# First q as fp32 by SyncE with a cast on chip, X of the last two batches turned by transposing DMAs, last stores on two queues, a new order

## The chip, the cores and the metric

The kernel runs on one core of a Trainium2 chip. The time is that of one execution on the device, in microseconds (us); lower is better. Of the kernel before there are three runs, and one profiled execution, from which the rows below are taken.

## The reference, cut to what matters

There are B = 4 batches of H = 8 heads, S = 768 tokens in 8 blocks of 96, and D = 64 columns a head. A matrix of 8x8 per head, normalised five times over rows and columns, mixes the blocks of k and v; each block of q then attends to one mixed block. The result x, with the heads side by side 512 wide, goes through a token mixer.

```python
for _ in range(5):                                  # sort_net, [B, H, 8, 8]
    P = exp(P - max(P, -1)); P = P / sum(P, -1); P = P / sum(P, -2)
k_sorted = einsum('bhij,bhjcd->bhicd', P, k_b)      # and v_sorted
attn = softmax(q_b @ k_sb^T / 8)                    # inside a block of 96
x = (attn @ v_sb), heads side by side               # [B, 768, 512]
wq, wk = x @ w_q, x @ w_k                           # 64 wide
mixed = (wq @ wk^T / 8) @ x
out = relu(mixed) @ w_out
```

## The kernel before, in words

The whole program is written out as units, and a string ORDER sets the order in which they are issued. A unit is a letter, a batch and a number: `P21:4` is unit P of batch 2, number 1, in PSUM bank 4. A capital letter is TensorE's work (PE in the rows); a small letter is the work that takes a bank away or stands between, with the engine behind the colon: A is ScalarE (ACT in the rows), D is VectorE (DVE), G is GpSimd (POOL), S is SyncE (SP). Each engine works its own units off in the order of the string, and stands still where the next one is not ready. The first lines of the string do the normalising (a, c, with B and n spreading the result to the mixing matrices M) and filling matmuls on zeros (Z). A batch then goes through these steps:

- lq, lk, lv load a whole batch of q, k or v: fp32 in memory, bf16 in the tiles Qn, Kn, Vn, the cast being done by the DMA. GpSimd issues them (L230). lp loads w_q and w_k (into a part of an output tile, until U and z have turned them), lo loads w_out.
- Q turns q of two heads, K mixes and turns k, V mixes v; q, k, v (small) copy the results to QT, KT and Vs. For batch 0 v goes through Y, y, F and f.
- R: six DMAs on SyncE's queue (L313) carry Vs to VT in another layout. All P units of the batch need all six.
- S and e are scores and exp, P the product with v, r and x the reciprocal (L375) and the division that writes X (L380). X has five parts, x0 to x4, of 14 (the last of 8) head-and-block units out of 64.
- T turns X of two heads with 8 matmuls against an identity, and t copies that to XT (the helper's L159 or L161): four units of each kind in a batch.
- J projects XT with w_q and w_k, j copies it to qkT, d copies half of its rows to qD (L407). W and w turn the part of w_k, G and g form w_k^T x, H and h the mixed rows with relu (L443 or L445), O is the product with w_out, o copies it to an output tile `ot`, and s stores it (L468, L471).

Four output tiles `ot` go round; two XT tiles and two X tiles alternate with the batches. SyncE's DMAs are issued one after the other in the order of the string, each when what it reads is there.

Of the kernel before, what the change touches and what calls it, by code (L numbers as in the profile page):

```python
# [17 lines left out]
ORDER = """
i02:D lq0 i00:G c00:D a01:A c01:D A00:0 a02:A:0 c02:D a03:A Z07:0 Q00:0 c03:D Q01:1 a04:A c04:D
q01:D:1 lk0 a05:A Q03:7 Q02:6 c05:D Z08:1 B00:1 n01:D:1 n00:D:1 Z04:2 K00:2 K01:4 q00:A:0 k00:A:2  # L20
n02:D:1 u00:D:1 i03:G n03:D:1 K03:0 K02:2 k01:A:4 k02:D:2 k03:A:0 S00:4 S02:0 e00:A:4 q02:D:6 lv0
e02:A:0 Y02:2 q03:D:7 Y01:4 lv1 Y00:6 y01:D:4 Y03:0 y02:A:2 S04:2 y00:A:6 n10:G n11:G y03:D:0 S03:4
F01:6 F00:7 e04:A:2 S01:0 F03:2 e03:A:4 e01:A:0 f01:D:6 f00:D:7 V11:3 V12:5 f03:D:2 F02:7 P00:0
v11:A:3 lk1 v12:D:5 S05:2 f02:A:7 e05:A:2 r00:D:0 V10:4 n21:G P01:6 K13:2 x00:D:0 r01:D:6 P02:0
x01:D:6 v10:A:4 r02:D:0 K10:4 K12:6 k13:A:2 P03:2 x02:D:0 lq1 r03:D:2 k10:A:4 K11:4 k12:D:6 T01:0
T00:1 lp Q11:6 k11:A:4 t00:A:1 S06:4 U00:7 R12:S Q12:1 R15:S e06:A:4 R11:S x03:D:2 P04:2 t01:D:0
Q13:0 Q10:4 q11:A:6 r04:D:2 z01:A:7 S12:5 q12:D:1 x04:D:2 q13:A:0 U01:7 q10:D:4 z02:D:7 T02:1 T03:0
e12:A:5 t02:D:1 t03:D:0 lq2 S11:2 S10:4 S13:6 Q22:1 Q21:0 e11:A:2 q21:D:0 Q23:2 e10:A:4 q22:D:1
J00:3 e13:A:6 R10:S R14:S n20:G R13:S S16:4 e16:A:4 S15:0 j00:D:3 P11:6 S14:3 J01:5 e15:A:0 q23:D:2
e14:A:3 P12:0 r11:D:6 lk2 K23:2 j01:A:5 x11:D:6 K21:6 r12:D:0 P13:4 k23:A:2 K20:2 x12:D:0 k21:A:6  # L30
r13:D:4 n30:G K22:0 Q20:6 x13:D:4 W00:7 k20:A:2 lv2 k22:A:0 P14:2 lq3 V20:4 V22:0 d00:S q20:D:6
r14:D:2 W01:7 x14:D:2 V21:2 T12:6 v22:D:0 t12:D:6 v20:A:4 P10:4 S25:0 v21:A:2 S26:2 T13:6 r10:D:4
w00:A:7 T11:7 x10:D:4 d01:S e26:A:2 S23:2 n31:G e25:A:0 Q30:4 G00:5 S21:0 t13:D:6 e23:A:2 t11:D:7
S24:6 lk3 e21:A:0 G01:5 Q31:3 lv3 e24:A:6 g00:D:5 Q33:2 q31:D:3 S22:0 T10:5 e22:A:0 S20:6 q33:D:2
t10:D:5 K32:2 R21:S K31:0 J11:5 k32:A:2 R20:S q30:D:4 R22:S H00:2 Q32:4 e20:A:6 k31:D:0 lo j11:D:5
h00:A:2 R23:S K30:0 R24:S H01:6 q32:D:4 K33:4 h01:A:6 R25:S k30:D:0 P21:2 J10:0 V31:6 k33:A:4 P23:4
j10:A:0 v31:A:6 r21:D:2 P22:0 d10:S x21:D:2 r23:D:4 V32:2 W10:6 v32:A:2 W11:6 O01:7 x23:D:4 w10:A:6
V30:4 r22:D:0 v30:A:4 x22:D:0 o01:D:7 O02:2 S34:0 o02:D:2 H02:6 e34:A:0 h02:D:6 S32:3 O03:5 e32:A:3
o03:A:5 P20:0 T21:7 P24:2 r20:D:0 T22:4 t21:A:7 G10:5 G11:5 x20:D:0 r24:D:2 d11:S g10:D:5 S36:6
R32:S t22:A:4 S30:0 e36:A:6 R35:S O00:4 x24:D:2 S31:5 e30:A:0 R30:S H11:2 H10:0 O05:7 o00:D:4 T20:4  # L40
h11:D:2 o05:D:7 e31:A:5 R34:S T23:5 h10:A:0 t20:A:4 t23:A:5 S35:2 e35:A:2 R31:S S33:0 H12:6 e33:A:0
s01:S O04:4 J20:5 O10:3 s00:S j20:A:5 R33:S P31:0 J21:5 o10:A:3 P32:2 h12:D:6 O15:6 r31:D:0 o04:D:4
j21:A:5 r32:D:2 o15:A:6 x31:D:0 P33:4 r33:D:4 O12:7 o12:A:7 P30:0 x33:D:4 s02:S O13:6 d20:S P34:4
W20:7 x32:D:2 W21:7 r34:D:4 d21:S o13:A:6 T31:2 w20:D:7 O14:3 t31:D:2 r30:D:0 O11:7 G20:2 x30:D:0
G21:2 o11:A:7 s10:S x34:D:4 T30:7 o14:A:3 g20:A:2 t30:A:7 T32:0 T33:1 t32:D:0 t33:D:1 H21:4 H20:2
H22:6 h20:D:2 s11:S J30:0 J31:1 h22:D:6 O20:2 j30:D:0 O21:3 h21:A:4 W30:0 O22:7 j31:A:1 d31:D
w30:A:0 W31:0 o22:D:7 w31:D:0 O24:1 o20:A:2 o21:A:3 o24:A:1 G30:7 G31:7 g30:D:7 O23:0 d30:D H30:4
h30:A:4 o23:D:0 H31:2 s12:S h31:D:2 O25:7 s20:S H32:0 s21:S O31:4 o25:A:7 h32:D:0 O30:7 o31:D:4
s22:S s31:S O314:0 O34:1 o314:A:0 s314:S o34:A:1 o30:D:7 O32:4 O35:0 o32:A:4 s30:S o35:A:0 s34:S
s32:S O315:7 o315:A:7 s315:S s35:S O33:4 o33:A:4 s33:S  # L50
"""


# [638 lines left out]
```

## Time and profile before

| what | us |
|---|---|
| median of three runs (lowest, highest) | 109.45 (108.54, 109.75) |
| span of the profiled execution, first to last instruction | 107.8 |
| PE busy | 89.2 |
| DVE busy | 72.2 |
| ACT busy | 68.6 |
| POOL busy | 25.6 |

The profile gives no other time for the profiled execution than its span. The median of the runs lies 1.65 us above that span, which stands for what lies around it. An engine's busy time counts its own instructions and not those that issue DMAs.

### The profile page before, as it was taken

Reading aid. Unit: us, or ns where it says so; the run is one execution under the profiler, and the core shown is the slowest. Engines: PE = TensorE matmul, PEld = TensorE weight load, DVE = VectorE, ACT = ScalarE, POOL = GpSimd, SP = SyncE. Lnnn points to the kernel's source line nnn. Section 1 sums busy time; section 2 is a strip of 40 time slices with the busy share of each in tenths; the row PEclk is TensorE's granted clock in tenths of the full one; section 3 lists DMA queues with packets and bytes.
Section 4 is the critical chain, followed back from the end, with each engine's and each line's share of the span. In section 5 each row is a group of like instructions: output and inputs, shape, how many; then the busy total and the mean of one; then the engine's idle time right before and its main releaser. Section 6 shows DMA issues by size and latency. Waiting matters only on the chain.

```text
span 107.8 us, 3532 instructions
## 1 busy us (share of the span) xinstructions
PE 89.2 (83%) x1495; PEld 63.0 (58%) x1503; DVE 72.2 (67%) x143; ACT 68.6 (64%) x99; POOL 25.6 (24%) x42
## 2 busy tenths in 40 slices
PE   0296997899989399989977799999999999999600
PEld 0126556798868377888845675856666755445300
DVE  2675655879987458979568499687299795587000
ACT  4223009999879848969959489999842664252600
POOL 5950009699089600000000000000000560000000
PEclk9999999999999999999999999999999999999995
DMA  0999999799999999999999933816060292447391
GB/s 3 106 197 205 203 203 205 81 191 205 209 236 247 223 199 204 209 209 205 236 253 223 179 78 102 270 70 222 6 231 0 78 406 109 198 179 270 121 376 39
DMA packets 18882, 19.37 MB, mean 180 GB/s; under 512 B 944, under 2 KB 17200, under 8 KB 18864
## 3 DMA queue, kind: packets, MB, share of 16 engines
q0 software_dynamic: 13296, 10.09, 61.7%
q1 hardware_dynamic: 5568, 9.03, 24.4%
q8 instruction: 12, 0.20, 0.7%
q14 instruction: 6, 0.05, 0.1%
HBM read 20.19 MB, written 6.29 MB: 246 GB/s over the span
## 4 chain that ended last, share of the span: by engine, by line
PE 50%; DMA 26%; ACT 7%; DVE 4%; POOL 4%; issue 3%; ACTq 0%; POOLq 0%; DVEq 0%
PE ps L155 50%; DMA Kn<-in_k_dram 19%; DMA Qn<-in_q_dram 7%; ACT E L351 3%; POOL M L251 2%; ACT KT L159 2%; DVE KT L161 2%; DVE M L251 1%; DVE QT L161 1%; POOL Vn L230 1%; POOL Qn L230 1%; ACT VT L159 1%; ACT ot L159 1%; DVE PTR L161 0%; ACTq L159 0%
## 5 line engine op out<-in xcount | busy, mean ns | idle before, releaser
L351 ACT ACTIVATE E<-ps 96x960 bf16<-96x960 f32 (+1 forms) x28 | 23.8, 909 | 3.1 <-PE ps L155 2.9
L155 PE MATMUL ps<-wo,mixT 128*128 128x512 bf16 (+1 forms) x97 | 22.8, 362 | 0.5 <-issue 0.2
L380 DVE TENSOR_TENSOR X<-ps,Rall 96x896 bf16<-96x896 f32 (+1 forms) x20 | 19.8, 1000 | 0.5
L159 ACT CAST KT<-ps 128x768 bf16<-128x768 f32 x14 | 10.7, 810 | 7.4 <-PE ps L155 7.3
L159 ACT COPY ot<-ps 128x512 f32<-128x512 f32 (+2 forms) x18 | 9.4, 541 | 8.4 <-PE ps L155 7.7
L155 PEld LDWEIGHTS <-mixT 128*128 128x128 bf16 x104 | 9.0, 98 | 8.3 <-issue 1.0
L155 PE MATMUL ps<-VT,E 96*128 96x65 bf16 x256 | 11.3, 193 | 1.4 <-ACT KT L159 1.3
L155 PEld LDWEIGHTS <-E 96*128 96x128 bf16 x256 | 9.9, 97 | 3.5 <-issue 1.6
L483 POOL CROSS_LANE_REDUCE s<-Rall 96x1 f32<-96x280 f32 x1 | 0.8, 757 | 46.8 <-DVE Rall L375 46.8
L155 PE MATMUL ps<-idb,Qn 128*64 128x128 bf16 x192 | 8.5, 244 | 3.1 <-DMA Qn<-in_q_dram 3.0
L251 POOL TENSOR_TENSOR M<-PTR,m_p 128x512 bf16<-128x512 bf16 x6 | 7.8, 1314 | 13.4 <-DVE PTR L161 9.5
L155 PEld LDWEIGHTS <-KT 64*128 64x128 bf16 (+1 forms) x288 | 8.4, 97 | 3.6 <-issue 2.2
L155 PEld LDWEIGHTS <-Qn 128*64 128x64 bf16 x192 | 7.2, 126 | 4.7 <-DMA Qn<-in_q_dram 4.2
L155 PE MATMUL ps<-QT,KT 64*128 64x96 bf16 x256 | 9.1, 204 | 0.7 <-ACT KT L159 0.7
L445 DVE TENSOR_SCALAR mixT<-ps 128x1024 bf16<-128x1024 f32 x7 | 8.5, 1221 | 1.2 <-PE ps L155 0.7
L161 DVE COPY QT<-ps 128x768 bf16<-128x768 bf16 x13 | 6.9, 547 | 3.3 <-PE ps L155 3.2
L375 DVE RECIPROCAL Rall<-ps 96x14 f32<-96x14 f32 (+1 forms) x20 | 4.6, 230 | 5.9 <-PE ps L155 4.7
L155 PE MATMUL ps<-M,Kn 128*64 128x128 bf16 x192 | 7.5, 221 | 1.1 <-DMA Kn<-in_k_dram 0.8
L159 ACT CAST Vs<-ps 128x1024 bf16<-128x1024 f32 x7 | 7.1, 1016 | 1.5 <-PE ps L155 1.5
L155 PE MATMUL ps<-fil 128*128 128x512 bf16 x18 | 6.5, 506 | 1.8 <-ACT m_p L173 1.6
L155 PEld LDWEIGHTS <-Kn 128*64 128x64 bf16 x192 | 6.1, 109 | 2.4 <-DMA Kn<-in_k_dram 0.9
L161 DVE COPY ot<-ps 128x512 f32<-128x512 f32 x9 | 6.0, 679 | 2.0 <-PE ps L155 2.0
(81 smaller groups left out, 132.7 us busy)
## 6 DMA issues: line engine op xcount, KB each, us to landing
out_dram<-ot SPq DMA_DIRECT2D x9, 512.0 KB, 3.1
Qn<-in_q_dram POOLq DMA_DIRECT2D x4, 768.0 KB, 11.4
Kn<-in_k_dram POOLq DMA_DIRECT2D x4, 768.0 KB, 12.7
Vn<-in_v_dram POOLq DMA_DIRECT2D x4, 768.0 KB, 15.1
VT<-Vs SPq DMA_DIRECT2D x18, 132.0 KB, 6.3
out_dram<-ot SPq DMA_DIRECT2D x4, 256.0 KB, 3.4
wo<-in_moe_w_out_dram POOLq DMA_DIRECT2D x1, 512.0 KB, 26.8
out_dram<-ot SPq DMA_DIRECT2D x4, 128.0 KB, 2.3
```

The lines of the kernel that those rows point to most:

```text
L155: nc.tensor.matmul(o, w, x, is_transpose=t, start=start, stop=stop, skip_group_check=True)
L159: nc.scalar.copy(o, i)
L161: nc.vector.tensor_copy(o, i)
L230: nc.gpsimd.dma_start(out=t[b % NIN][:, h0:h1].rearrange("p h r d -> p h (r d)"), in_=src[b, h0:h1].rearrange("h (p r) d -> p h (r d)", p=P))
L251: ENG[e].tensor_tensor(out=M[b % 2][:, h0:h0 + hn], in0=src.unsqueeze(2).to_broadcast([P, hn, SP, NB]), in1=m_p.unsqueeze(1).unsqueeze(3). ...
L351: nc.scalar.activation(E[b % 2][:, n, 0:2 * w * BLK].rearrange("p (t a c) -> p a t c", a=2, c=BLK), PS[0:BLK, bank:bank + 2, 0:w * BLK].re ...
L375: nc.vector.reciprocal(Rall[:, b, n, :, 0:w], avps(bank, w)[:, :, :, D])
L380: nc.vector.tensor_mul(xo.rearrange("p (a t d) -> p a t d", a=2, d=D), avps(bank, w)[:, :, :, 0:D], Rall[:, b, n, :, 0:w].unsqueeze(3).to_ ...
L445: nc.vector.tensor_relu(o, i)
L483: g.tensor_reduce(s1[:, 1:2], rv, axis=AX.XYZWC, op=ALU.max)
```

## The change

- Two DMAs on SyncE's queue bring q of batch 0 as fp32, four heads each, into the two XT tiles, which nothing else uses yet. Four units z1 cast two heads each into Qn: z10, z11 and z12 on GpSimd, z13 on ScalarE. The unit lq0 is gone.
- Batches 2 and 3 have no T and t units any more (eight of each). Units D20, D21, D30 and D31 are transposing DMAs on SyncE's queue instead: each turns half of X (four heads: 96 partitions x 16 pieces of 128 columns, bf16) into half of XT. D20 and D30 read parts x0 to x2, D21 and D31 read x2 to x4.
- Three of the last eight stores (s34, s35, s30) are issued by ScalarE.
- The order is new. Fewer Z matmuls stand in it: 9 and 6 where there were 7, 8 and 4. lp stands ahead of the first k.

```diff
-SPQ = False
+SPQ = 2
 ORDER = """
-i02:D lq0 i00:G c00:D a01:A c01:D A00:0 a02:A:0 c02:D a03:A Z07:0 Q00:0 c03:D Q01:1 a04:A c04:D
+i00:G A00:6 i02:D c00:D lp a01:A c01:D Z09:0 lk0 i03:G z10:G z11:G Q01:2 lv0 a02:A:6 c02:D Q00:3
...
-s32:S O315:7 o315:A:7 s315:S s35:S O33:4 o33:A:4 s33:S
+o314:D:6 s35:A o32:D:4 o31:A:7 o33:D:2 O30:6 s315:S s314:S s32:S o30:A:6 s33:S s31:S s30:A
 """
...
     if SPQ:
-
-        q32 = XT[0].rearrange("p t s -> p (t s)").bitcast(FP32).rearrange("p (h r d) -> p h r d", r=R6, d=D)
-        nc.sync.dma_start(out=q32.rearrange("p h r d -> p h (r d)"),
-                          in_=q[0, 0:H // 2].rearrange("h (p r) d -> p h (r d)", p=P))
+        q32 = [x.rearrange("p t s -> p (t s)").bitcast(FP32).rearrange("p (h r d) -> p h r d", r=R6, d=D) for x in XT]
+        for m in range(SPQ):
+            hs = slice(m * H // 2, (m + 1) * H // 2)
+            nc.sync.dma_start(out=q32[m].rearrange("p h r d -> p h (r d)"),
+                              in_=q[0, hs].rearrange("h (p r) d -> p h (r d)", p=P))
...
     def copy(e, o, i):
         if e == "A":
             nc.scalar.copy(o, i)
+        elif e == "G":
+            nc.gpsimd.tensor_copy(o, i)
         else:
             nc.vector.tensor_copy(o, i)
...
         if b == 1:
-            copy(e, Qn[0][:, 2 * n:2 * n + 2], q32[:, 2 * n:2 * n + 2])
+            m, o = divmod(2 * n, H // 2)
+            copy(e, Qn[0][:, 2 * n:2 * n + 2], q32[m][:, o:o + 2])
```

The unit D was in the kernel before, without an item in the order that calls it:

```python
    def u_D(b, n, e, bank):
        ENG[e].dma_start(out=XT[b % 2][:, 2 * n:2 * n + 2, :].rearrange("p k (i c) -> p (k i) c", c=BLK),
                         in_=X[b % 2][:, 2 * n:2 * n + 2].rearrange("c k i m -> c (k i m)"), transpose=True)
```

SyncE's queue from the R units of batch 2 (VT_85) to the first stores, before; qD_95 is for batch 2, VT_86 for batch 3:

```order
L313 DMA VT_85<-Vs_84 16x8x528 x6
L407 DMA qD_96<-qkT_94 64x384 x2
L313 DMA VT_86<-Vs_84 16x8x528 x5
L468 DMA out_dram<-ot_104 128x1024
L468 DMA out_dram<-ot_103 128x1024
L313 DMA VT_86<-Vs_84 16x8x528
L468 DMA out_dram<-ot_105 128x1024
L407 DMA qD_95<-qkT_93 64x384 x2
```

The same stretch of SyncE's queue now, and on to the first store of batch 1 (ot_106); XT_91 is for batch 2, XT_92 for batch 3:

```order
L315 DMA VT_85<-Vs_84 16x8x528 x6
L410 DMA qD_96<-qkT_94 64x384 x2
L315 DMA VT_86<-Vs_84 16x8x528
L389 DMA_TRANSPOSE XT_91<-X_89 128x16x96 x2
L315 DMA VT_86<-Vs_84 16x8x528 x5
L471 DMA out_dram<-ot_105 128x1024
L410 DMA qD_95<-qkT_93 64x384
L471 DMA out_dram<-ot_104 128x1024
L471 DMA out_dram<-ot_103 128x1024
L410 DMA qD_95<-qkT_93 64x384
L389 DMA_TRANSPOSE XT_92<-X_90 128x16x96 x2
L471 DMA out_dram<-ot_106 128x1024
```

Two transposing DMAs now stand between the first and the second R unit of batch 3, and two more behind the stores of batch 0.

GpSimd behind the first loads of q and k and the clearing of tiles, before, up to k of batch 1:

```order
L217 MEMSET Rall 96x4x2x3
L230 DMA Vn_75<-in_v_dram 128x8x384
L230 DMA Vn_76<-in_v_dram 128x8x384
L251 TENSOR_TENSOR M_108<-PTR,m_p 128x512 x2
L230 DMA Kn_73<-in_k_dram 128x8x384
```

GpSimd behind the same clearing, now (ahead of it stand the weights and the first k):

```order
L219 MEMSET Rall 96x4x2x3
L161 CAST Qn_69<-XT_91 128x768 x2
L232 DMA Vn_75<-in_v_dram 128x8x384
L161 CAST Qn_69<-XT_92 128x768
L232 DMA Vn_76<-in_v_dram 128x8x384
L232 DMA Kn_73<-in_k_dram 128x8x384
L232 DMA Qn_70<-in_q_dram 128x8x384
L253 TENSOR_TENSOR M_110<-PTR,m_p 128x512
```

The first two casts now stand ahead of the first load of v, the third ahead of the second, and k and q of batch 1 are issued ahead of the multiplications that make M, behind which they stood.

## Rows read from the trace of the kernel before

**Rows 1.** Chain that ended last, in order of time: start us, us, what.
```profile
1.27 7.75 DMA Qn<-in_q_dram
...
34.28 20.70 DMA Kn<-in_k_dram
...
55.02 2.42 PE ps L155 x44
...
101.63 0.59 ACT ot L159
```

**Rows 2.** Windows: us; busy us (x) of PE, PEld, DVE, ACT, POOL; clock, DMA, GB/s.
```profile
15.50:55.00 39.50, 34.75 (x833) 29.40 (x832) 30.69 (x53) 33.57 (x43) 16.75 (x17) 1.00 1.25 206
55.00:60.00 5.00, 3.63 (x74) 2.52 (x75) 2.84 (x4) 4.25 (x5) 0.00 (x0) 1.00 1.25 231
60.00:101.60 41.60, 41.06 (x509) 25.92 (x515) 29.89 (x46) 26.38 (x41) 3.23 (x7) 1.00 0.46 157
```

**Rows 3.** Timeline of PE: two T units of batch 2, two S units behind them.
```profile
72.49 0.84 PE L155 MATMUL ps<-idb,X 96*128 96x96 bf16 x16
73.27 0.60 PE L155 MATMUL ps<-QT,KT 64*128 64x96 bf16 x20
```

**Rows 4.** Timeline of PE: J, P, O; three H and what follows; two G.
```profile
76.84 0.81 PE L155 MATMUL ps<-XT,wqk 128*128 128x384 bf16 x4
77.50 0.60 PE L155 MATMUL ps<-VT,E 96*128 96x65 bf16 x14
77.94 1.03 PE L155 MATMUL ps<-wo,mixT 128*128 128x512 bf16 x4
78.80 0.60 PE L155 MATMUL ps<-VT,E 96*128 96x65 bf16 x14
...
86.30 0.28 PE L155 MATMUL ps<-qkT,Ab 64*128 64x256 bf16 x1
...
87.06 1.47 PE L155 MATMUL ps<-XT,wqk 128*128 128x384 bf16 x8
...
92.25 1.06 PE L155 MATMUL ps<-X,wk 96*64 96x256 bf16 x16
```

**Rows 5.** Timeline of PE: its longest wait behind the last load of k.
```profile
59.94 0.60 PE L155 MATMUL ps<-VT,E 96*128 96x65 bf16 x14 [1.34 <-ACT KT L159]
```

**Rows 6.** Tile Vn: issue ns min/median/max, first and last start; below, issue to landing.
```profile
L230 POOL DMA_DIRECT2D Vn<-in_v_dram x4: 883/890/939, 5.0 to 35.2; - x4
...
DMA to landing us min/median/max: 11.7/15.1/25.1
```

**Rows 7.** The page: GB/s that the DMA engines moved, in 40 equal slices.
```profile
GB/s 3 106 197 205 203 203 205 81 191 205 209 236 247 223 199 204 209 209 205 236 253 223 179 78 102 270 70 222 6 231 0 78 406 109 198 179 270 121 376 39
```

**Rows 8.** Timeline of POOL: multiplications for M, a load, an operation on 280 columns.
```profile
16.25 2.57 POOL L251 TENSOR_TENSOR M<-PTR,m_p 128x512 bf16<-128x512 bf16 x2 [9.51 <-DVE PTR L161]
18.76 0.94 POOL L230 DMA_DIRECT2D Kn<-in_k_dram  x1
...
85.48 0.93 POOL L484 TENSOR_SCALAR Rall<-Rall 96x280 f32<-96x280 f32 x1 [1.06 <-DVE X L380]
```

**Rows 9.** Timeline of PE: the first K units.
```profile
15.54 1.94 PE L155 MATMUL ps<-M,Kn 128*64 128x128 bf16 x48
```

**Rows 10.** Tile VT: R's issue on SyncE's queue, ns min/median/max; below, issue to landing.
```profile
L313 SPq DMA_DIRECT2D VT<-Vs x18: 546/588/1314, 25.0 to 72.1; - x18
...
DMA to landing us min/median/max: 2.3/6.3/7.6
```

**Rows 11.** Timeline of SyncE's queue: the six R units of batch 1.
```profile
25.02 5.13 SPq L313 DMA_DIRECT2D VT<-Vs  x6
```

**Rows 12.** Timeline of DVE: the reciprocals of two parts of X in a row.
```profile
62.18 0.24 DVE L375 RECIPROCAL Rall<-ps 96x14 f32<-96x14 f32 x1 [0.17 <-PE ps L155]
...
63.46 0.23 DVE L375 RECIPROCAL Rall<-ps 96x14 f32<-96x14 f32 x1
```

**Rows 13.** Timeline of SyncE's queue, from 103.8 us: the last store.
```profile
103.71 0.41 SPq L471 DMA_DIRECT2D out_dram<-ot  x1
```

More of the change, by code (lines that the diff above doesn't have):

```diff
@@ L15 @@
 NMIX = 2
-SPQ = False
+SPQ = 2
 ORDER = """
-i02:D lq0 i00:G c00:D a01:A c01:D A00:0 a02:A:0 c02:D a03:A Z07:0 Q00:0 c03:D Q01:1 a04:A c04:D
[L20 to L46, printed above, removed]
@@ L47 @@
-w30:A:0 W31:0 o22:D:7 w31:D:0 O24:1 o20:A:2 o21:A:3 o24:A:1 G30:7 G31:7 g30:D:7 O23:0 d30:D H30:4
-h30:A:4 o23:D:0 H31:2 s12:S h31:D:2 O25:7 s20:S H32:0 s21:S O31:4 o25:A:7 h32:D:0 O30:7 o31:D:4
-s22:S s31:S O314:0 O34:1 o314:A:0 s314:S o34:A:1 o30:D:7 O32:4 O35:0 o32:A:4 s30:S o35:A:0 s34:S
-s32:S O315:7 o315:A:7 s315:S s35:S O33:4 o33:A:4 s33:S
+i00:G A00:6 i02:D c00:D lp a01:A c01:D Z09:0 lk0 i03:G z10:G z11:G Q01:2 lv0 a02:A:6 c02:D Q00:3
+a03:A c03:D U00:1 a04:A z13:A Q03:5 c04:D q00:A:3 z12:G Q02:6 a05:A q01:A:2 z01:D:1 c05:D lv1
@@ new lines @@
+q03:A:5 q02:A:6 U01:1 lk1 Z06:3 B00:7 z02:A:1 u00:A:7 n03:D:7 K03:0 n00:D:7 K00:2 k03:A:0 n01:D:7
+k00:A:2 lq1 n02:D:7 K01:4 n11:G k01:D:4 K02:6 Y00:0 Y01:2 k02:A:6 lq2 y00:D:0 Y02:4 y01:A:2 Y03:6
+S01:0 F01:2 y03:D:6 F00:3 S00:6 y02:A:4 n10:G f01:D:2 S02:4 f00:D:3 F02:2 F03:3 n21:G f02:D:2
+e01:A:0 V11:0 e00:A:6 lk2 e02:A:4 f03:D:3 S06:6 S03:4 S05:2 v11:D:0 n20:G e06:A:6 e03:A:4 P00:6
+r00:D:6 e05:A:2 V10:0 V12:4 S04:2 v10:A:0 e04:A:2 x00:D:6 v12:D:4 P01:6 r01:D:6 K11:0 K12:4 K13:2
+R11:S x01:D:6 k11:A:0 K10:0 k12:D:4 k13:A:2 P02:6 P04:2 T00:4 k10:A:0 r02:D:6 t00:A:4 Q13:5 Q10:0
@@ new lines @@
+x02:D:6 q13:D:5 R10:S q10:A:0 r04:D:2 Q12:1 x04:D:2 lv2 q12:D:1 lq3 Q11:7 P03:4 S16:2 T01:6 r03:D:4
+q11:A:7 S14:0 e16:A:2 R13:S lk3 S15:2 e14:A:0 e15:A:2 x03:D:4 t01:D:6 T03:4 R14:S T02:5 S13:6
+t03:D:4 e13:A:6 t02:D:5 S11:0 S12:2 e11:A:0 n31:D J00:4 Q21:5 Q22:6 Q20:7 Q23:0 R15:S j00:A:4 R12:S
+e12:A:2 W00:1 q21:D:5 P11:2 q22:A:6 q20:D:7 P12:4 S10:6 e10:A:6 n30:G q23:D:0 r11:D:2 J01:0 K23:6
+x11:D:2 r12:D:4 x12:D:4 K20:2 j01:A:0 k23:A:6 K21:4 W01:1 K22:6 d01:S k20:D:2 lv3 d00:S k21:A:4
+P14:4 k22:A:6 w00:D:1 r14:D:4 S20:2 S26:0 e26:A:0 P13:6 e20:A:2 S25:0 x14:D:4 r13:D:6 V22:4 x13:D:6
@@ new lines @@
+V20:2 V21:6 v22:D:4 e25:A:0 T12:0 lo G00:1 v20:A:2 v21:D:6 S22:2 S21:4 e22:A:2 e21:A:4 t12:D:0 G01:1
+P10:6 T11:0 S23:2 g00:D:1 S24:4 r10:D:6 Q33:1 x10:D:6 T13:6 q33:D:1 t11:D:0 t13:D:6 e23:A:2 H01:2
+Q32:7 e24:A:4 Q30:1 H02:4 q32:D:7 T10:0 h01:A:2 q30:D:1 R24:S h02:A:4 H00:2 h00:A:2 t10:D:0 Q31:1
+R21:S R20:S R23:S q31:D:1 J11:6 K33:0 R22:S k33:A:0 K30:4 K31:2 j11:D:6 k31:A:2 K32:6 k30:D:4 S35:0
+R25:S k32:D:6 J10:5 P21:2 e35:A:0 S36:6 S32:0 j10:A:5 e36:A:6 d10:S P23:4 V31:6 e32:A:0 r21:D:2
+x21:D:2 v31:A:6 P22:2 r23:D:4 x23:D:4 V32:0 P20:4 r22:D:2 d11:S x22:D:2 v32:A:0 r20:D:4 V30:6 W10:2
@@ new lines @@
+W11:2 x20:D:4 P24:0 O01:3 w10:A:2 G10:2 G11:2 r24:D:0 x24:D:0 S30:4 o01:D:3 v30:A:6 S34:6 e34:A:6
+g10:D:2 R34:S O00:3 D20:S O02:2 H11:6 e30:A:4 D21:S H10:0 R31:S R35:S h11:A:6 H12:4 o00:D:3 h12:A:4
+h10:D:0 O05:3 O04:6 R32:S o04:A:6 S33:0 o05:D:3 S31:4 o02:D:2 R33:S J20:7 J21:6 R30:S e31:A:4
+j21:A:6 j20:D:7 e33:A:0 O03:3 W20:2 P31:4 W21:2 o03:D:3 P34:0 P30:6 O10:3 r31:D:4 x31:D:4 r34:D:0
+s02:S d20:S w20:A:2 s01:S o10:A:3 P32:4 r30:D:6 O11:2 x30:D:6 o11:A:2 s00:S r32:D:4 P33:6 x32:D:4
+O12:3 d21:S r33:D:6 G20:4 x33:D:6 G21:4 O14:6 D30:S o12:A:3 x34:D:0 g20:D:4 H22:0 H21:2 H20:4 O15:7
@@ L51 @@
+h21:D:2 o14:A:6 h20:D:4 O13:6 O23:2 D31:S o15:D:7 O21:3 J31:7 J30:4 s10:S o13:A:6 h22:D:0 O22:5
+j31:D:7 W31:6 j30:A:4 W30:0 O20:4 w31:A:6 w30:A:0 G30:0 s12:S o23:D:2 d31:A o20:D:4 G31:0 O24:1
+o21:A:3 d30:D g30:D:0 H32:6 o22:A:5 s11:S H31:2 s21:S h32:A:6 H30:4 O25:0 O314:6 o24:D:1 o25:A:0
+h30:D:4 h31:D:2 O34:7 O35:0 o34:A:7 s20:S s34:A O315:5 o315:D:5 O32:4 O33:2 O31:7 s22:S o35:A:0
+o314:D:6 s35:A o32:D:4 o31:A:7 o33:D:2 O30:6 s315:S s314:S s32:S o30:A:6 s33:S s31:S s30:A
 """
```

## The prediction

> **What bounds the kernel now.** I read the chain of waits first. It begins with the first q on its way, landing at 9.02 us, and its longest single piece is a load of k: 20.70 us, up to 54.98. From 55.02 on it is nearly all TensorE until the last copy at 101.63 [rows 1]. So there are two stages, and the windows show what each is limited by [rows 2]. From 15.5 to 55 us the loads are the limit: TensorE works 34.75 of 39.50 us and is short of work for 4.75, while the DMA engines move 206 GB/s almost evenly; ScalarE with 33.57 and VectorE with 30.69 us have no great reserve. From 60 to 101.6 us TensorE works 41.06 of 41.60 us: whatever is taken from it there shortens the run, as long as nothing else comes late. Between the two lies one wait of TensorE of 1.34 us for a copy of k [rows 5]. Behind the last copy (101.63 + 0.59 = 102.22) the last store is issued only at 103.71 [rows 1, 13], since SyncE is still busy with stores ahead of it.
>
> **T and t of batches 2 and 3 go.** Two T units take TensorE from 72.49 to 73.27, 0.39 each [rows 3]. Eight are left out, all of them in the stretch behind 55 us where TensorE is the limit: 8 x 0.39 = 3.1 us. The eight copies lie on engines that are not the limit there (26.38 and 29.89 of 41.60 us, [rows 2]) and count nothing. Term: **-3.1**, bounds -2.8 and -3.5.
>
> **The order.** Counted through the order, the units H00, H01, H02, Q32 and J11 now stand ahead of the first K of batch 3; they stood behind it. Three H take 0.76 us, a J 0.66 [rows 4], a Q, of twelve short matmuls, I count 0.5 (a quarter of the 48 of K, which take 1.94, [rows 9]): 1.9 us of TensorE that moves into a stretch in which it was idle for 4.75 [rows 2]. Term: **-1.9**, and zero if TensorE reaches that place late. The wait of 1.34 us [rows 5] was for a K unit's copy; now all four K units stand together with S35 and J10 behind them, and the copies of k have these to hide behind. Behind them V31 needs the last v, which landed at about 35.2 + 25.1 = 60.3 us [rows 6]. The units from the first K to V31 sum to 4.0 us (55.0 + 4.0 = 59.0), so a wait of up to 1.3 takes the place of the one that goes if the loads end no earlier. I take the loads to end somewhat earlier (next part) and count **-1.0**, bounds 0 and -1.3.
>
> **The start.** Both halves of q as fp32 come through SyncE beside k through GpSimd. The trace shows no such load. By the stores, which move fp32 and reach 406 GB/s in a slice where the casting loads hold about 205 of what is written, that is half of what they read [rows 7], the fp32 q costs what it cost; if what counts is the bytes written, it takes 1.57 MB / 205 GB/s = 7.7 us instead of 3.8, and all loads end 3.8 us later. I take the first, because 406 is the nearest row in kind of transfer (SyncE's queue, fp32 at both ends). The casts on GpSimd are not in the trace either. The multiplication for M takes 1.29 us for 512 columns, the one on fp32 0.93 for 280 [rows 8]; for 768 columns that gives 1.9 to 2.6 us, and I take 2.0. With the first half of q there at 7, z10 and z11 end at 11, and only then is the first v issued, landing its first bytes after 12 us; q and k, two loads of 3.8 us from about 3.5 on, are through at about 11. So the queue of loads runs dry for some 1.5 us there. Before, it ran dry too: the slice from 18.9 to 21.6 us moves 81 GB/s, because the next k was issued only at 18.76, behind the multiplications [rows 7, 8]; that is (1 - 81/205) x 2.7 = 1.6 us, and goes now that k and q of batch 1 are issued ahead of them. The two cancel, and SyncE's earlier first byte leaves a small gain. The third cast stands behind the first v on GpSimd, so Q02 comes at about 14, and the filling matmuls, the spreading matmuls B00 and the first K behind it: first K at 17 instead of 15.54 [rows 9]. The queue of ScalarE has some slack to take that back; I count **+1.0**, bounds 0 and +3.8.
>
> **The transposing DMAs.** Nothing in the trace turns data in a DMA. Nearest in queue and kind (SBUF to SBUF, from SyncE) is R. One R moves 135 KB, holds SyncE for 0.59 us in the median and lands 2.3 us after its issue at best, 1.7 behind the end of it [rows 10]; six of them held SyncE 5.13 us, 0.86 each, while loads were running [rows 11]. A D moves 393 KB, three R's worth. Lowest: as one R, 0.59. By bytes: 1.8 to 2.6. By pieces: R writes 128 runs, 4.6 ns each; D writes 2,048 runs of 192 bytes, 9.4 us. I take **2.2 us** of SyncE and 1.7 more to land: bytes, since the row is nearest to it in amount, and between R's two prices.
>
> Where this falls due: counted in batch 2 from the end of P24, TensorE has O01, two G, S30, S34, O00, O02, three H, O05, O04, S33, S31 ahead of J20, which reads XT: five O at 0.86, two G at 1.0 together, three H 0.76, four S at 0.22, 6.9 us [rows 3, 4] (a row's busy time holds some 0.17 of tail beside the next row, as P's 0.60 against 0.44 up to the next start shows, so two S take 0.43). VectorE does four parts of X in a row, 1.28 us each [rows 12], and is through with x20 1.6 us behind P24. D20 is issued there, D21 2.2 us later, SyncE is free at 6.0 and D21 lands at 7.7: TensorE stands 0.8 us. Behind the two D stand five R of batch 3, for which P31 waits: 6.0 + 5 x 0.59 + 1.7 = 10.7, while P31 is due at 9.3 + 0.8: another 0.6. In batch 3, counted from the end of P33, TensorE has six O, two G and three H ahead of J31, 6.9 us again; D30 is issued at 0.7, D31 at 2.9, landing at 6.8: nothing. Term: **+1.4**; with 0.59 it is 0, and above 2.25 us a D each further microsecond costs 4, two in each batch: 4d - 7.5.
>
> [...]
>
> **The last stores.** s30 is now issued by ScalarE right behind its own copy. Before, 103.71 - 102.22 = 1.5 us lay between them [rows 1, 13]; some time of issue stays. Term: **-1.0**, bounds 0 and -1.4.
>
> **Sum.** -3.1 - 1.9 - 1.0 + 1.0 + 1.4 - 1.0 = -4.6. The profiled execution spans 107.8; 103.2 are left. The median of the runs lies 1.65 above that span: 104.8 us.
>
> **Rivals.**
> 1. *SyncE is held by the D units* (slower). If a D costs far more than R by bytes, J20, then P31 behind the R units, then J31 stand. Without this term the sum is -6.0, so it decides from 4d - 7.5 = 6.0, d = 3.4 us, on. At 4.7, half of the price by pieces, stalls are 11.3 and the time 109.45 - 6.0 + 11.3 = 114.8. For it: D writes short runs, and SyncE is one queue, with R behind D. Against it: R by bytes. [...]
> 2. *The start is late*: casts at 2.6 us, or the fp32 load at 7.7. All loads, and with them V31, end 2 to 3.8 us later; the part of the order (-1.9) is lost too. 104.8 + 2.9 = 107.7, still faster.
> 3. *D lands early everywhere and the loads close up*: no stall, -1.4, and no late start, -1.0: 102.4.
> 4. *The change does not do what it says*, the stage behind 55 us not being TensorE's any longer: VectorE has r, x, h and o there. Its sum there (29.89 of 41.6) would have to grow by 8, and the order shows nothing of that size; the T term is lost only in part, 106.5. I count this with the forecast's upper half.
>
> **How the numbers follow.** The forecast with its neighbours (103.4 to 106.9) has 0.45, rival 3 and better 0.20, rival 2 up to 108.3 0.12, a result within 1% 0.08, rival 1 0.15. A change of 1% (1.1 us) is about what a measurement of this kernel can tell from none. Faster by more: 0.45 + 0.20 + 0.12 = 0.77; within: 0.08; slower: 0.15. For 8 in 10 the range takes in rival 3 down to 101.5 and goes up to 110.0, leaving out most of rival 1 and a little below.
>
> **What would show it.** In the profile after: X's PE transposes at 64 instead of 128; from the first K of batch 3 to the last matmul some 40 us instead of 46.5; SyncE's queue with a transposing DMA of about 2.2 us each; TensorE waiting under 1 us each before J20 and P31, and not before J31; no slice at 81 GB/s, a thin one near 11 us; the last store issued within 0.5 us of the last copy. Wrong it would be made by a D above 3.4 us, or by a last v that lands behind 62 us.

## The result and the profile after

The changed kernel takes 104.02 us in the median of 4 runs (103.57 to 105.11), the kernel before 109.0 (4 runs) on the same chip: a ratio of 0.9635, interval 0.9525 to 0.9745. The prediction said 104.8, so time and sign were right; several terms under the sum were not. Executions of one kernel differ by more than 2% (before: 107.34 to 109.75 us), and since the longer ones are left out of the ratios but not of the medians, the gain is read from the ratio: 3.65% of some 108 us, 3.9 us.

The profiled execution took 103.57 us and spans 101.4, which is 6.4 less than the span before. That is more than the gain, for two reasons. The span before, 107.8, goes with some 109.6 us and not with 108: in group 1 below, executions of that kernel with spans of 107.7 and 107.8 took 109.51 and 109.65 us. And the time now lies 2.2 us above the span (103.57 against 101.4), where it lies about 1.8 above it for the kernel before in group 1, and also for q_back, which loads the first q as before: some 0.35 us more lie outside the span.

The page after, slices of the span in tenths (TensorE's granted clock) and GB/s:

```profile
PEclk9999599999999999999999999999999999999999
...
GB/s 18 294 329 215 203 204 205 203 204 204 204 226 251 247 200 205 205 214 207 201 250 248 223 106 1 98 211 225 310 205 241 167 280 239 270 111 338 378 318 99
```

The slice at 81 GB/s [rows 7] is gone, and there is no thin slice near 11 us in its place: the queue of loads no longer runs dry. New is a slice at half clock: 0.50 from 10 to 12.5 us.

The chain that ended last, after, in order of time:

```profile
1.68 7.09 DMA XT<-in_q_dram
8.82 0.83 POOL Qn L161
...
11.33 17.33 DMA Qn<-in_q_dram
...
50.24 7.99 DMA VT<-Vs
58.27 2.01 PE ps L155 x50
...
74.48 5.74 DMA out_dram<-ot
80.30 0.59 ACT ot L159
...
97.39 0.59 ACT ot L159
```

Where a load of k stood [rows 1], there is now a load of q, and behind 50 us an R unit (the last of batch 2), whose transfer takes 7.99 us beside the last loads. The last copy ends at 97.98 instead of 102.22.

The stretch behind the first K of batch 3, parted at V31, before and then after (us; busy us of the engines; clock, DMA, GB/s):

```profile
55.02:61.03 6.01, 4.67 (x91) 3.29 (x91) 3.19 (x6) 4.25 (x5) 0.00 (x0) 1.00 1.24 227
61.03:101.55 40.52, 40.03 (x492) 25.15 (x497) 29.54 (x45) 26.38 (x41) 3.23 (x7) 1.00 0.44 156
```

```profile
54.21:59.66 5.45, 4.18 (x105) 3.24 (x105) 3.02 (x5) 3.45 (x7) 0.00 (x0) 1.00 1.11 207
59.66:97.37 37.71, 36.63 (x392) 21.65 (x394) 28.47 (x44) 19.87 (x30) 3.23 (x7) 1.00 0.69 218
```

So the 6.4 us of span lie in three places. V31 starts at 59.66 instead of 61.03: -1.4. From V31 to the end of the last copy it is 38.32 us instead of 41.19: -2.9, with TensorE busy 36.63 instead of 40.03. From there to the end of the span 3.4 instead of 5.6: -2.2. A second profile of the same kernel (control, below) gives +0.7, -3.3 and -2.2. The second part holds: the old order takes 41.35 us there in tail_alone and 41.19 in loads_early (both below). The first does not. The third is too large, because in the profile before one store held SyncE's queue for 2.29 us, and the DMA engines moved 0 to 12 GB/s from 100.5 to 102 us:

```profile
99.36 2.29 SPq L471 DMA_DIRECT2D out_dram<-ot  x1
```

In tail_alone the longest such issue is 1.52 us and the end takes 4.8; in loads_early, with the same last stores as before, the eight last issues take 4.89 us together (before 5.66) and the end takes 4.7. So the end shrank by 1.3 to 1.4 us.

The transposing DMAs and the casts, tiles X and XT after (ns min/median/max, first and last start; below, issue to landing of D):

```profile
L389 SPq DMA_TRANSPOSE XT<-X x4: 1290/1439/1912, 64.2 to 79.9; - x4
L161 POOL CAST Qn<-XT x3: 822/822/827, 5.7 to 8.8; 128x768 bf16<-128x768 f32 x3
```

```profile
DMA to landing us min/median/max: 3.6/3.7/3.8
```

SyncE's queue and TensorE where J20 (70.99), P31 (73.32) and J31 (84.92) stand, after; the second is the timeline of PE:

```profile
64.23 3.31 SPq L389 DMA_TRANSPOSE XT<-X  x2
67.64 3.21 SPq L315 DMA_DIRECT2D VT<-Vs  x5
```

```profile
70.99 1.47 PE L155 MATMUL ps<-XT,wqk 128*128 128x384 bf16 x8
...
73.32 0.60 PE L155 MATMUL ps<-VT,E 96*128 96x65 bf16 x14
...
84.92 1.30 PE L155 MATMUL ps<-XT,wqk 128*128 128x384 bf16 x7
```

Two D hold SyncE 3.31 us, 1.65 each with the time between, and no row carries a wait in brackets: TensorE does not stand for D anywhere.

### The profile page after: what moved, and what is told of

It reads as the page before. It is cut to its first block, busy times and chain, and to the rows that moved or that the text cites. A ratio compares the mean times of both kernels' runs of the same rounds, so it can differ in the third digit from the quotient of the medians.

```text
span 101.4 us, 3380 instructions
## 1 busy us (share of the span) xinstructions
PE 86.9 (86%) x1428; PEld 59.3 (59%) x1435; DVE 75.0 (74%) x142; ACT 65.4 (65%) x94; POOL 25.7 (25%) x43
## 4 chain that ended last, share of the span: by engine, by line
PE 42%; DMA 38%; DVE 6%; ACT 3%; POOL 2%; issue 2%; SPq 2%; DVEq 0%; ACTq 0%
PE ps L155 42%; DMA Qn<-in_q_dram 17%; DMA VT<-Vs 8%; DMA XT<-in_q_dram 7%; DMA out_dram<-ot 6%; DVE X L383 4%; DVE Rall L378 1%; ACT ot L159 1%; SPq L315 1%; ACT E L354 1%; POOL Kn L232 1%; POOL Qn L161 1%; POOL Vn L232 1%; ACT KT L159 1%; DVE ot L163 1%
## 5 line engine op out<-in xcount | busy, mean ns | idle before, releaser
L159 ACT COPY ot<-ps 128x512 f32<-128x512 f32 (+1 forms) x13 | 7.0, 554 | 10.4 <-PE ps L155 7.7
L163 DVE COPY ot<-ps 128x512 f32<-128x512 f32 (+2 forms) x14 | 8.9, 648 | 4.5 <-PE ps L155 2.8
L159 ACT CAST KT<-ps 128x768 bf16<-128x768 f32 x13 | 9.8, 804 | 2.1 <-PE ps L155 2.0
L155 PE MATMUL ps<-idb,Qn 128*64 128x128 bf16 x192 | 7.5, 233 | 3.0 <-POOL Qn L161 1.7
L155 PEld LDWEIGHTS <-Qn 128*64 128x64 bf16 x192 | 6.2, 117 | 5.2 <-POOL Qn L161 2.6
L448 DVE TENSOR_SCALAR mixT<-ps 128x1024 bf16<-128x1024 f32 x6 | 7.2, 1219 | 2.1 <-ACT ot L159 1.2
L253 POOL TENSOR_TENSOR M<-PTR,m_p 128x512 bf16<-128x512 bf16 x5 | 6.6, 1314 | 5.5 <-PE ps L155 3.1
L163 DVE CAST KT<-ps 128x768 bf16<-128x768 f32 x7 | 6.5, 952 | 1.1 <-PE ps L155 1.0
L446 ACT ACTIVATE mixT<-ps 128x1024 bf16<-128x1024 f32 x6 | 5.9, 1022 | 1.4 <-PE ps L155 1.3
L155 PE MATMUL ps<-XT,wqk 128*128 128x384 bf16 x32 | 6.2, 328 | 0.0
```

The lines of the kernel that those rows point to most:

```text
L155: nc.tensor.matmul(o, w, x, is_transpose=t, start=start, stop=stop, skip_group_check=True)
L253: ENG[e].tensor_tensor(out=M[b % 2][:, h0:h0 + hn], in0=src.unsqueeze(2).to_broadcast([P, hn, SP, NB]), in1=m_p.unsqueeze(1).unsqueeze(3). ...
L446: nc.scalar.activation(o, i, ACT.Relu)
L448: nc.vector.tensor_relu(o, i)
```

## The experiments

Each was run in 5 rounds beside the kernel before, in three groups on three chips, where before took 109.15 us (group 1), 109.03 (group 2) and 108.45 (group 3); ratios to before are what is compared across groups.

**The changed kernel again (control, group 1).** No edit.

> The changed kernel once more, as the level for the runs beside it on the same chip. Every theory expects 104.0 us and a ratio of 0.96 to the kernel before; the spread against the first measurement says how far differences between runs can be trusted.

104.93 us, ratio 0.976 (0.9695 to 0.9824). The gain is 2.4 to 3.65% on two chips, 2.6 to 3.9 us.

**T instead of D in the new order (t_back, group 1; t_back2, group 2).** t_back puts the T units of batches 2 and 3 with their copies back and takes D out; t_back2 does the same with PSUM banks that are free at that point (and O22 ahead of J31).

```
- D20:S … D21:S … D30:S … D31:S
+ T20:4 T21:5 T22:0 T23:1 …   (t_back)
+ T20:7 T21:4 T22:5 … T23:7 … T30:4 T31:5 T32:3 … T33:7   (t_back2)
```

> The changed kernel with the four transposing DMAs undone: eight T units on TensorE and eight copies on ScalarE and VectorE for batches 2 and 3 again, in its new order. Theory (TensorE is the limit behind the last loads, so its 8 x 0.39 us come back whole): 3.1 us slower than the control. Rival (VectorE and the copies are the limit there by now, TensorE has gaps of its own): under 1.5 us slower, and more idle time of TensorE does not come with it.

> T and t of batches 2 and 3 on TensorE, ScalarE and VectorE again, as in t_back, but in banks that are free by then: in t_back a T unit stood in a bank that an h unit still had to read, TensorE waited 1.59 us there, its granted clock went to half, and eight matmuls of O took 3.25 us instead of 1.9; so that run priced more than T. Theory (TensorE's 8 x 0.39 us come back, and the copies now stand in the way of the relu copies): 3 to 4 us slower than the changed kernel, 107.5 to 109. Rival (the new order has no room for T wherever it stands): again 5 us or more slower.

t_back: 110.97 us, 1.0226 (1.0132 to 1.0321). In it T20 waited 1.59 us for a bank, so it prices the banks too. t_back2: 110.87 us, 1.0179 (1.0091 to 1.0268). The new order with T is slower than the old one. D is worth 4.2% of the kernel before in it against the control and 5.4% against the first measurement, some 4.5 to 5.9 us, more than the 3 to 4 expected. The timeline of PE in t_back2:

```profile
72.31 1.19 PE L156 MATMUL ps<-idb,X 96*128 96x96 bf16 x24
...
73.85 0.50 PE L156 MATMUL ps<-idb,X 96*128 96x96 bf16 x8
...
87.73 1.52 PE L156 MATMUL ps<-idb,X 96*128 96x96 bf16 x32
...
89.86 1.89 PE L156 MATMUL ps<-wo,mixT 128*128 128x512 bf16 x8 [0.61 <-ACT XT L160]
```

The T units are 1.19 + 0.50 + 1.52 = 3.2 us of TensorE, as forecast. Of the rest the trace shows a wait of 0.61 for the copy of XT and one of 0.25 for that of qkT; what else it is was not shown.

**D instead of T in the old order (d_alone, group 2).** The kernel before, with T20 to T33 and their copies out and D20, D21, D30, D31 put behind the x units that they read.

```
- T21:7 … T22:4 t21:A:7 … T20:4 … T23:5 … T31:2 … T30:7 … T32:0 T33:1 …
+ x20:D:0 D20:S … x24:D:2 D21:S … x30:D:0 D30:S … x34:D:4 D31:S
```

> The kernel before with one part of the change alone: transposing DMAs for T and t of batches 2 and 3, all else in the old order. In batch 2 some 10 us of TensorE's work lie between the last part of X and J20, in batch 3 only three H units (0.76 us) between x34 and J30. Theory (a DMA of 1.65 us of issue that lands 3.7 us after its start is free where it has cover and costs what is missing where it has none): batch 2 gives 1.5 us, batch 3 gives 1.5 and loses about 4 waiting for J30: 0 to 1.5 us slower than before. Rival (T's time on TensorE is all that counts): 3.1 us faster.

117.54 us, 1.0704 (1.0619 to 1.079): 7.6 us slower, where at most 1.5 were expected. SyncE's queue, and TensorE's waits in the same profile, which is of an execution of 120.1 us:

```profile
69.42 1.51 SPq L385 DMA_TRANSPOSE XT<-X  x1
70.99 0.57 SPq L406 DMA_DIRECT2D qD<-qkT  x1
71.65 1.27 SPq L312 DMA_DIRECT2D VT<-Vs  x2
73.02 1.55 SPq L385 DMA_TRANSPOSE XT<-X  x1
74.66 1.84 SPq L312 DMA_DIRECT2D VT<-Vs  x3
...
77.71 0.78 SPq L312 DMA_DIRECT2D VT<-Vs  x1
```

```profile
73.46 0.27 PE L154 MATMUL ps<-qD,Ab 64*128 64x256 bf16 x1 [2.15 <-DMA qD<-qkT]
...
81.72 0.61 PE L154 MATMUL ps<-VT,E 96*128 96x65 bf16 x14 [2.99 <-DMA VT<-Vs]
...
94.74 0.48 PE L154 MATMUL ps<-XT,wqk 128*128 128x384 bf16 x2 [1.46 <-DMA XT<-X]
...
97.84 0.48 PE L154 MATMUL ps<-XT,wqk 128*128 128x384 bf16 x1 [2.62 <-DMA XT<-X]
```

d11 (the qD row) and all six R of batch 3 stand behind D20 on SyncE, and D20 waits for x20. So a wait of one D reaches qD, VT and, in batch 3, XT itself, which has little work ahead of J30 there. Together the four waits take 9.2 us, while T's 3.1 are saved. The clock was lower behind the second and the fourth: the mean granted clock was 0.76 from 80 to 85 us and 0.90 from 85 to 90, 0.63 from 95 to 100 and 0.69 from 100 to 105, and 1.00 from 55 to 80 and from 90 to 95. Same D, about the same price of issue (1.5 us), opposite sign: the order makes the gain, and in this one place in the old order the transfer loses it; no other place, and no other queue, was run. SyncE held by D is what rival 1 feared, but it is held by D's wait for X here, not by a dear D.

**Each D twice (d_twice, group 2).** The changed kernel; behind each D a second one of the same half into a tile that nobody reads any more.

```
+ Xd = Kn[1]…[:, n * 2 * S:(n + 1) * 2 * S]
+ ENG[e].dma_start(out=Xd…, in_=X[b % 2][:, 2 * n:2 * n + 2]…, transpose=True)
```

> The changed kernel with every transposing DMA followed by a second one of the same half of X into a tile that nothing reads any more: the cost of D on SyncE's queue doubled. Theory (D holds SyncE for 1.65 us, and the five R of batch 3 behind it are what P31 waits for): the first J20 stands by 0.2 us, P31 by some 2.5 us, batch 3 by 0.2: 2 to 3 us slower than the changed kernel. Rival (D is hidden with room to spare, as the short waits in the changed kernel suggest): within 0.7 us. Second rival (the transfers themselves collide with stores and R in the DMA engines): more than 4 us slower.

110.61 us, 1.015 (1.0074 to 1.0225): by the ratios 4.2 us above the control and 5.6 above the first measurement; 2 to 3 were expected. SyncE's queue in d_twice, then its timeline of PE and a window (column behind POOL: clock):

```profile
65.66 1.91 SPq L389 DMA_TRANSPOSE XT<-X  x1
67.66 1.31 SPq L392 DMA_TRANSPOSE Kn<-X  x1
69.08 1.55 SPq L389 DMA_TRANSPOSE XT<-X  x1
70.68 1.84 SPq L392 DMA_TRANSPOSE Kn<-X  x1
72.62 3.43 SPq L315 DMA_DIRECT2D VT<-Vs  x5
```

```profile
73.06 1.14 PE L155 MATMUL ps<-XT,wqk 128*128 128x384 bf16 x6 [0.15 <-DMA XT<-X]
...
77.99 0.59 PE L155 MATMUL ps<-VT,E 96*128 96x65 bf16 x14 [2.76 <-DMA VT<-Vs]
...
79.55 1.90 PE L155 MATMUL ps<-wo,mixT 128*128 128x512 bf16 x4
```

```profile
80.00:85.00 5.00, 5.00 (x50) 2.91 (x50) 3.97 (x9) 1.62 (x3) 0.75 (x1) 0.76 0.36 137
```

Four D hold SyncE from 65.66 to 72.52, the R units start 5 us later than in the changed kernel, and P31 (77.99) waits 2.76 us for VT. The prediction's 4d - 7.5 with d = 2 x (72.52 - 65.66) / 4 = 3.4 gives 6.2: near the size measured, and the run falls to the slower side where the prediction had put that point, at 3.4. Its places do not hold: of the waits that it adds up, J20 stands 0.15 us, P31 2.76 and J31 not at all, much as this run's own expectation had it. Part of the rest is clock: behind P31's wait its mean was 0.76 from 80 to 85 us, and four matmuls of O at 79.55 took 1.90 us, against 1.03 [rows 4] where it was 1.00 [rows 2].

**q in fp32 undone (q_back, group 1).** First q through GpSimd with its cast in the transfer, as the other loads; the four casts on chip left out.

```
- SPQ = 2
+ SPQ = 0
- … Z09:0 lk0 i03:G z10:G z11:G Q01:2 … z13:A … z12:G …
+ i00:G lq0 A00:6 … Z09:0 lk0 i03:G Q01:2 …
```

> The changed kernel with q of batch 0 loaded by GpSimd with the cast in the DMA, as before, the casts z10 to z13 left out, all else in the new order. Theory (the new order of the loads closes the gap in the load queue, SyncE's fp32 q only shifts the first microseconds): within 0.6 us of the control. Rival (SyncE's early fp32 q is what lets the loads end earlier): 1 us or more slower, with the first K of batch 3 later by as much.

104.95 us, 0.977 (0.972 to 0.982): the control's time. The new way of loading the first q is worth nothing.

**The loads' new place alone (loads_early, group 2).** The kernel before, k and q of batch 1 issued right behind the second load of v.

```
- … q03:D:7 Y01:4 lv1 Y00:6 … v11:A:3 lk1 … x02:D:0 lq1 r03:D:2 …
+ … q03:D:7 Y01:4 lv1 lk1 lq1 Y00:6 …
```

> The kernel before with one part alone: k and q of batch 1 issued by GpSimd right behind the second v, ahead of the multiplications that make M. Theory (the gap of the load queue from 18.9 to 21.6 us, 1.6 us of transfers, delays all later loads, and the last k and v set the pace up to 60 us): all loads 1.5 us earlier, 1 to 1.5 us faster. Rival (by then ScalarE and VectorE set the pace, the loads only look like the limit): within 0.5 us, with TensorE idle for ScalarE instead of the loads.

107.17 us, 0.9892 (0.9832 to 0.9952): 1.2 us by the ratio, 0.5 to 1.8 by its interval. Its window over the former thin slice:

```profile
18.90:21.60 2.70, 2.44 (x57) 2.27 (x56) 2.19 (x4) 2.70 (x5) 2.57 (x4) 1.00 1.32 203
```

203 GB/s instead of 81: the loads no longer pause, and V31 comes at 59.14, 0.7 us earlier than in tail_alone. The prediction's 1.6 us for this pause lies within the interval.

**The last stores (one_queue, group 1; tail_alone, group 3).** one_queue: the changed kernel with s34, s35 and s30 on SyncE again. tail_alone: the kernel before with s33 on ScalarE.

```
- s34:A … s35:A … s30:A
+ s34:S … s35:S … s30:S     (one_queue)
- s33:S
+ s33:A                     (tail_alone)
```

> The changed kernel with the three last stores s34, s35 and s30 on SyncE's queue again. Theory (SyncE issues the last stores one after the other and is late with the last one): 1.0 to 1.5 us slower than the control, all of it behind the last copy. Rival (the stores end when their data has landed, whoever issues them): within 0.3 us.

> The kernel before with its very last store, s33, issued by ScalarE instead of SyncE, and nothing else changed. Theory from the run with one queue: 0.6 us less than the kernel before. Rival, the step as it was forecast: the whole time in which the last store stands behind the others on SyncE goes, 1.0 to 1.4 us less.

one_queue: 105.57 us, 0.9807 (0.9751 to 0.9864), 0.6 above the control with overlapping intervals. tail_alone: 108.72, 1.0017 (0.9978 to 1.0057), no gain, where both theories had one. Its timeline of ScalarE at the end, and windows behind it:

```profile
100.64 0.58 ACT L159 COPY ot<-ps 128x512 f32<-128x512 f32 x1 [0.55 <-PE ps L155]
101.25 0.41 ACTq L471 DMA_DIRECT2D out_dram<-ot  x1
```

```profile
101.00:102.00 1.00, 0.00 (x0) 0.00 (x0) 0.00 (x0) 0.22 (x1) 0.00 (x0) 1.00 1.06 393
102.00:103.00 1.00, 0.00 (x0) 0.00 (x0) 0.00 (x0) 0.00 (x0) 0.00 (x0) 1.00 1.07 397
```

The store is issued 0.03 us behind its copy, as meant, and then the DMA engines still move 393 and 397 GB/s for two us: not the issue ends this run but the bytes that are left. In the changed kernel the same windows behind its last copy (98 to 99, 99 to 100 us) show 318 and 215: less is left there. From the last copy to the end of the span one_queue takes 3.75 us, the control 3.4 and the old order 4.7 to 4.8, so about 1 us of the shorter end comes from the new order of the last units and at most 0.4 from the second queue.

**TensorE's stand-still at the start (warm, group 3).** Meant to fill TensorE's wait for the cast q. The two digits of a Z unit are a batch and a count, so the kernel that ran has four idle matmuls ahead of Q01 instead of nine, and three new ones behind U00. It tests the opposite of its expectation: a longer stand-still.

```
- Z09:0 … U00:1 a04:A
+ Z14:0 … U00:1 Z03:6 a04:A
```

> The changed kernel with 14 instead of 9 idle matmuls ahead of Q01 and six new ones behind U00, so that TensorE does not stand still in the 1.7 to 2.0 us in which it waits for the cast q. Theory that the stand-still is what the half clock of 10 to 17 us follows on: the granted clock stays near 1.0 through the first 20 us, the first units of that stretch take some 1 to 1.5 us less, and the kernel about 1 us less than the changed kernel, near 103.3. Rival, that the first stage waits for its loads whatever the clock: within 0.4 us of the changed kernel, 104 to 105.

104.25 us, 0.9536 (0.9465 to 0.9607). Its timeline of PE, and its window and that of the changed kernel's profile at 10 us (column behind POOL: clock):

```profile
7.54 1.49 PE L155 MATMUL ps<-idb,Qn 128*64 128x128 bf16 x24 [4.07 <-POOL Qn L161]
```

```profile
10.00:12.50 2.50, 2.50 (x30) 1.56 (x29) 2.26 (x10) 2.25 (x5) 2.39 (x3) 1.00 1.31 203
```

```profile
10.00:12.50 2.50, 2.28 (x28) 1.73 (x26) 2.23 (x11) 2.31 (x5) 2.22 (x3) 0.50 1.32 204
```

TensorE stood 4.07 us and kept the full clock; in the changed kernel it stood 1.74, in the control 2.01, and half clock followed. In s00_first and d_twice, whose starts are the changed kernel's, it stood 1.85 and 1.7 and the clock stayed full (1.00 from 5 to 20 us in s00_first; in d_twice this is an estimate: its mean of 0.984 over 108.8 us leaves 1.7 us missing, and the 0.89 from 75 to 80 and 0.76 from 80 to 85 us already make 1.75). So the theory that this stand-still brings the half clock falls. Whether the time fell at all cannot be told: against s00_first in the same group it is 0.7 us less, with overlapping intervals, and the control, whose interval lies wholly above, ran on another chip.

**The store s00 earlier (s00_first), and both edits (warm_s00), group 3.**

```
- … s01:S o10:A:3 … o11:A:2 s00:S r32:D:4
+ … R30:S s00:S e31:A:4 …
```

> The changed kernel with the store s00 on SyncE right behind the transposing transfer R30 instead of four steps later, behind s02, s01 and the transfer d20. Theory that the 2.72 us which the copy o12 waits for this store slow the H units by 0.4 us and that these reach the end: 0.4 us less than the changed kernel, and the wait of o12 under 1 us. Rival, that the H units have slack there: no difference to be told from none, and the wait shorter all the same.

> The changed kernel with both edits, the idle matmuls ahead of Q01 and behind U00 and the early store s00. By the two theories 1.4 us less than the changed kernel, near 102.9, the fastest of all; if only the clock counts 1 us less; by both rivals the time of the changed kernel, 104 to 105.

104.99 us, 0.9603 (0.9528 to 0.9679), and 103.7 us, 0.9519 (0.9455 to 0.9583). The copy o12 no longer waits for the store: in s00_first it stands at 80.83 with 0.72 us for TensorE instead of 2.72 for the store in the changed kernel (second row).

```profile
80.83 0.59 ACT L159 COPY ot<-ps 128x512 f32<-128x512 f32 x1 [0.72 <-PE ps L155]
```

```profile
80.30 1.07 ACT L159 COPY ot<-ps 128x512 f32<-128x512 f32 x2 [2.72 <-DMA out_dram<-ot]
```

Yet from V31 (61.71) to the end of the last copy (100.12) s00_first takes 38.41 us, the changed kernel 38.32, control 37.91, and one_queue, whose clock fell behind V31 as that of s00_first did (0.83 from 60 to 70 us; s00_first 0.87 from 60 to 62.5 and 0.50 from 62.5 to 65), 38.11: the rival holds, there was slack. So the chain's 5.74 us for a store [chain after, 74.48] cost nothing, although the chain ran through it. Both edits together had the lowest ratio of all, but its interval overlaps that of the changed kernel's first run, and the control was on another chip: a faster version is not shown.

## Why the prediction was right, point by point

**T and t go, -3.1: the price was right.** X's transposes by TensorE are 64 instead of 128, and put back, T took 3.2 us of TensorE. From V31 on the time fell by 2.9 (control: 3.3) and TensorE's busy time by 3.4. But by the order, H02, P23, S32, S35 and S36 left this stretch too, another 1.35 us by the prices of [rows 3, 4]. So 4.5 us of work went and 2.9 to 3.4 us of time: T's part of the fall can't be told apart.

**The transposing DMAs, +1.4: mis-sized, 0.** The step that failed is "2.2 us of SyncE and 1.7 more to land": it was 1.65 and 3.7 from issue to landing (d's median 1.44). In 4d - 7.5 that is below zero, and the trace has no wait at J20, P31 or J31. With d doubled the formula's size nearly held, its places did not. Bytes were nearly the right scale, and the estimate by pieces, 9.4 us a D, with rival 1's half of it, 4.7, was too long: D moves 2.9 times the bytes of an R and is issued in 1.44 us against R's 0.59 [rows 10].

**The order, -1.9, and the wait for k's copy, -1.0: not found where they were forecast.** This is the step that failed by most. V31 should have come earlier by both. In ten profiles with the new order it starts at 59.66 (after) to 61.80 (q_back), in the control at 61.70; before at 61.03, in tail_alone, whose order there is the same, at 59.87. From the first K of batch 3 to the last matmul the prediction had some 40 us instead of 46.5; it is 43.2 (97.37 - 54.21). The wait of 1.34 us for KT [rows 5] did go, but another took its place, for the last R of batch 2, in front of P21; the timelines of PE in the changed kernel, and in s00_first:

```profile
58.27 0.61 PE L155 MATMUL ps<-VT,E 96*128 96x65 bf16 x14 [0.48 <-DMA VT<-Vs]
```

```profile
60.32 0.61 PE L155 MATMUL ps<-VT,E 96*128 96x65 bf16 x14 [1.92 <-DMA VT<-Vs]
```

In one_queue, q_back, d_twice and t_back2 it is 1.79 to 1.83 us. The prediction looked at loads and copies there and not at R, which is issued at 50.2 and lands 8 us later beside the last loads; before, at most 7.6 [rows 10]. Besides, three S units and P23, 1.1 us by the prices of [rows 3, 4], now stand ahead of V31; the prediction had not taken them off its 1.9, and this part comes back behind V31. What the order did pay is the other way round: it is the one in which D fits. With T it is 1.8% slower than the old order, with D 2.4 to 3.65% faster, while the old order with D is 7% slower. Counted by units, 5.0 us of TensorE's work left the stretch behind the first K of batch 3, by busy time 3.9 (44.70 to 40.81); where the other 1.1 us went stays open.

**The start, +1.0: mis-sized, about 0.** Casts on GpSimd took 0.82 us, not 2.0; the step that scaled them from the multiplications [rows 8] was wrong by more than two. So the loads did not run dry near 11 us, and the first K came at 14.98 (control: 15.77) instead of 17. The pause in the loads, in the sum as cancelled by that, was a true gain of 1.2 in the old order (loads_early); in the new one it does not show, since V31 comes no earlier. The kernel with the fp32 load took as long as the one with the casting load (control 104.93 us, q_back 104.95), as chosen.

**The last stores, -1.0: size nearly right, cause wrong.** The end shrank by 1.3 to 1.4 us, but putting the last store on ScalarE gave nothing in the old kernel and 0.6 at most in the new one; the rest lies in the new order of the last units. The 1.5 us between last copy and last store [rows 1, 13], on which the term rests, held in part a store's issue of 2.29 us in that one execution; there the last store's issue ends 1.9 us behind the last copy (104.12 against 102.22), in loads_early 1.1 (101.46 against 100.33).

**The sum, -4.6, against 2.6 to 3.9 measured by the ratios.** Beside the profile of tail_alone (107.78 us, and a kernel that takes as long as the one before) the parts are, after and (control): up to V31 -0.2 (+1.8), from there to the last copy -3.0 (-3.4), the end -1.4 (-1.4), outside the span +0.35; together -4.2 (-2.6), which is what these executions differ by. The missing gain up to V31 (2.9 counted) is largely made up by the missing stalls (1.4), the missing late start (1.0) and the longer fall of the end (0.4 more): a total near the right one over errors of both signs, and so in part luck. The time of 104.8 came out near the measured one also because 107.8, from which the sum starts, goes with a longer time than that of most executions. Rival 1 did not come to pass, but SyncE held by D cost the most of all seen here: 7.6 us in d_alone and 4.2 to 5.6 in d_twice.

## What to carry to other kernels

The work that moved from TensorE to SyncE's queue took that queue's time in order, 3.31 and 3.23 us for two D each: list what stands behind it and when each of these is due, then set the order, since the same transfer was worth some 5 us in one order and its move cost 7.6 in another. When TensorE stands for such a transfer, look at the clock behind the wait as well (0.76 and 0.63 in the windows behind two waits of d_alone). At a kernel's end, see whether the DMA engines are busy behind the last copy (393 and 397 GB/s in tail_alone) before moving a store's issue, and in more than one profile. A piece on the chain that ended last, like the 5.74 us for a store here, may still have slack of its own; a run without it (s00_first) told.

## What the runs showed of the hardware

- A transposing DMA within SBUF of 96 by 2,048 bf16 (393 KB) held SyncE's queue 1.29 to 1.91 us and landed 3.6 to 3.8 us after issue in the changed kernel (after); in d_alone up to 2.23 and 4.4, in d_twice up to 1.91 and 4.8.
- A cast of 128 x 768 from fp32 to bf16 took 0.82 us on GpSimd and 0.83 on ScalarE (after).
- TensorE's granted clock fell in the starts of after (0.50 from 10 to 12.5 us), control (0.50 from 10 to 17.5), one_queue (0.89 in the mean from 0 to 15) and t_back (0.81), but not in those of s00_first (1.00 from 5 to 20) and d_twice (the estimate above, from its mean of 0.984), the same program there, nor of warm (1.00 from 5 to 20), with the longest stand-still, 4.07 us. Behind the wait before P21 it fell where that was 1.66 us (warm_s00: 0.50 at 60 to 62.5 us), 1.81 (one_queue: 0.83 at 60 to 70), 1.83 (t_back2: 0.66 at 60 to 65) and 1.92 (s00_first: 0.50 at 62.5 to 65), and stayed at 1.00 where it was 0.48 (after), 0.59 (control) and 0.76 (warm), but also where it was 1.79 (q_back) and 1.8 (d_twice). From V31 on warm_s00 and s00_first still needed 37.9 and 38.4 us, against 37.9 to 38.3 in the others. What decides it stays open.
- Loads of the first q as fp32 by SyncE left 0.35 us more between the span and the time: 2.15 to 2.23 us in the changed kernel and the control, 1.78 to 1.86 in q_back.
